# Turning attention probabilities on VectorE, through DRAM, for 24 of 32 head pairs

## The chip, the cores and the metric

One core of a Trainium2 chip runs the whole program. The metric is the device time of one execution in microseconds (us), as the median of several runs. The engines are TensorE (PE, with PEld for its weight loads), VectorE (DVE), ScalarE (ACT), GpSimd (POOL) and SyncE (SP), which only issues DMAs here.

## What is computed

Two attentions per head are added up and go through a gated spatial unit (batch 8, 8 heads, 576 tokens, head width 64):

```python
q_d, k_d, v_d = means over groups of 4 tokens        # 144 rows each
out_d  = softmax(q_d @ k_d.T / 8) @ v_d               # "downsampled"
mask   = abs(i - j) < 4                               # a band of 7 tokens
out_l  = softmax(where(mask, q @ k.T / 8, -1e9)) @ v  # "local"
x      = repeat(out_d, 4) + out_l                     # heads side by side: 576 x 512
h      = relu(x @ w_in);  u, v = h[:, :512], h[:, 512:]
v_n    = (v - mean(v)) / sqrt(var(v) + 1e-6)          # over channels
out    = (u * (w_spatial @ v_n + b_spatial)) @ w_out
```

## The kernel before

The work goes in head pairs (two heads on 2 x 64 partitions), four pairs per batch and 32 in all, and in one block of matrix products per batch, `gated(b)`, which needs the four pairs of its batch. The weights are loaded, decoded from 64-bit floats and split into two f16 halves at the start, beside the first pairs.

A pair (`attention(n)`) loads q and k transposed (`qk`), sums groups of four tokens (`sum1`, `sum2`, on DVE or POOL), and makes scores in PSUM. The local scores go in ten windows (`WS`) of 64 queries by 64 keys, two windows stacked on 128 partitions, five blocks of two: 128 x 640. `QB` says which queries of a window are used. The band mask is either added by two matmuls (PE) or by DVE. Then come the maximum, the subtraction on DVE (or folded into ten small exponentials of ACT), the exponential, the sum, its inverse and the normalisation. The downsampled scores are 144 x 144 per head, in three parts of 112 partitions, with the same steps (names with `d`).

The product with the values needs the probabilities with keys on partitions. So PE turns them: `turn` makes five 128 x 128 transposes (against `ident`) into a PSUM buffer `pa`, which ACT copies to `probT`; `turn_d` makes six transposes of 112 x 100 (against `perm`) into two PSUM buffers `pm`, which ACT copies to `pdT` (a single buffer). Then `values` and `values_d` multiply with v, DVE adds both results (`both`), and the sum is split into two f16 halves `x`. From pair 8 on (`MERGE`) the two kinds of scores are one piece of PE's order, and `values_d` with `values` another.

Every piece of work is handed to a planner (`plan.op`) with its engine, its cost in ns, the buffers that it reads and writes, and a rank. `Plan.run` goes through the program in its own time, and on each engine takes, among the pieces that can start within `NEAR` ns, the one with the lowest rank; that gives the order in which each engine's instructions are written. A DMA is given 1900 ns, then `kb` ns one after another, then 900 ns. Each engine, SP too, works in this fixed order, so an instruction that waits holds all behind it. `ON` picks for each pair, by a letter (P POOL, D DVE, A ACT, T PE), where a step runs; past the end of a string its last letter holds. Until 110 us the planner fills PE's gaps with matmuls that compute nothing (`warm`).

Of the kernel before, what the change touches and what calls it, by code (L numbers as in the profile page):

```python
# [8 lines left out]
F32 = mybir.dt.float32  # L9
# [67 lines left out]
class Plan:  # L77
# [61 lines left out]
    def run(self, near=150.0, stay=0.0, dma=(1900.0, 900.0), emit=True):  # L139
# [17 lines left out]
        while left:  # L157
# [122 lines left out]
MRANK = {"V": [[-120.813, 103.137], [-373.166, -785.223], [-588.287, 86.439], [-457.053, -295.554], [-271.069, 53.075],  # L280
            [-161.929, 7.172], [-384.75, 67.584], [1.753, -86.54]],
        "U0": [[-381.018, 507.475], [-225.844, -398.15], [392.079, 353.99], [415.277, -261.891], [-69.09, -16.703], [-362.251,
            -497.795], [59.314, -190.411], [573.297, -308.684]],
        "S0": [[631.14, 127.639], [-206.013, -184.383], [299.174, 561.899], [-372.357, 30.262], [381.875, 239.103], [33.324,
            19.169], [-136.587, -125.569], [104.744, -531.737]],
        "U1": [[66.951, 205.966], [432.921, 80.243], [202.58, -320.842], [-584.875, -261.385], [85.111, -539.421], [-290.079,
            -515.53], [-73.151, -407.568], [-105.893, -362.577]],
        "O0": [[170.632, -34.982], [-172.469, 696.573], [159.95, -390.053], [-841.668, -359.026], [22.932, -667.87], [-349.956,
            231.605], [321.827, -73.48], [-54.093, -578.395]],
        "S1": [[-122.247, -1002.997], [272.521, 179.124], [-502.627, -34.942], [83.425, -28.324], [193.115, 251.294], [212.725,  # L290
            -514.576], [-0.655, 14.458], [254.101, -410.908]],
        "O1": [[-425.021, 297.386], [239.962, 469.652], [56.568, -208.235], [-194.872, 129.628], [-641.125, -6.104], [281.584,
            274.929], [184.644, 89.516], [19.298, 376.248]]}
EVICT = 456.633
WRANK = {"WV load": [31.22, -21.921, 242.309, 4.474],
        "WV decode": [350.543, -287.444, -567.367, 661.466],
        "WV bound": [-83.736, 162.235, 909.503, 36.755, -835.361],
        "WV split": [-201.598, 11.031, -341.826, -1007.43],
        "WU load": [-364.293, 427.826, 390.089, -59.831],
        "WU decode": [387.574, -316.232, 1019.795, 459.568],  # L300
        "WU bound": [1425.684, -228.293, 245.85, 118.051, 725.352],
        "WU split": [-187.848, -607.313, -258.771, -328.661],
        "WSP load": [289.708, -579.107, 622.627, -316.354, 744.76],
        "WSP bound": [397.382, 106.669, -930.598, 200.751, 873.332, -382.338],
        "WSP split": [-150.625, -91.686, 309.424, 430.824, -1165.74],
        "WO load": [201.774, -325.888, 429.457, 987.307],
        "WO decode": [137.835, 619.019, -225.889, -8.083],
        "WO bound": [-64.148, 457.463, -289.1, 18.247, -58.582],
        "WO split": [620.04, -563.746, 894.059, 1022.164]}
NEAR = 104.496  # L310
STAY = 26.882
# [21 lines left out]
def tile_kernel(ctx, tc, qk, vw, v4, w_in, wT, bsp, w_out, out, emit=True):  # L333
# [75 lines left out]
    more = const.tile([P, 2, 2 * FF], F32, name="more")  # L409
# [9 lines left out]
    places("kd", 3, [P, 2, G], F32)  # L419
# [26 lines left out]
    places("mb", 6, [P, FF], F32)  # L446
# [254 lines left out]
    def attention(n):  # L701
# [16 lines left out]
        sb, kb = plan.buf("sum"), plan.buf("kd")  # L718

# [4 lines left out]
        def sum2():  # L724
            side(s2).tensor_tensor(kb.ap, sb.ap[:, :, ::2], sb.ap[:, :, 1::2], op=ALU.add)
# [7 lines left out]
        merge = n >= MERGE  # L733
# [73 lines left out]
        def scores_d():  # L807

            q = kb.ap.rearrange("p x g -> p (x g)")
            for h, a, i, e in ((0, 0, 0, 0), (0, 1, 1, 0), (1, 1, 0, 2), (1, 2, 1, 2), (0, 2, 0, 1), (1, 0, 1, 1)):  # L810
                r, o = slice(h * 64, h * 64 + 64), slice(i * 64, i * 64 + 64)
                nc.tensor.matmul(third(e)[o], q[r, a * 48:a * 48 + 64], kb.ap[r, 1], start=True, stop=True)
# [74 lines left out]
        def turn_d():  # L889
            for kc in range(2):  # L890
                v = ptd[kc].ap[:KEYS, :3 * PD].rearrange("p (a q) -> p a q", a=3)
                for a in range(3):
                    nc.tensor.transpose(v[:, a, :], ed.ap[:PD, a, kc], perm[:PD])
# [358 lines left out]
```

## Time and profile before

| | us |
|---|---|
| median of 3 runs | 579.25 (578.70 to 579.31) |
| span of the profiled execution | 577.2 |
| PE busy | 553.0 (96%) |
| DVE busy | 411.4 (71%) |
| ACT busy | 376.0 (65%) |
| POOL busy | 186.0 (32%) |

The median is 2.05 us above the profiled span. [...] A row of a timeline says start, duration, engine, line, operation, output and inputs, and how many instructions are merged. A row by line says how many instructions, their busy time, the mean ns of one, and the idle time before them. Matmuls overlap, so that PE's next instruction can start before the last has ended. The granted clock falls short of 1.00 only in the first 50 us (0.93).

### The profile page before, as it was taken

The page shows a single profiled execution, that of the slowest core. Times are in us where ns is not written, and L with a number is a line of the kernel's source. Part 1 is how long each engine was busy: PE and PEld are TensorE (multiplying, and loading weights), DVE is VectorE, ACT ScalarE, POOL GpSimd, SP SyncE. Part 2 cuts the span into 40 slices and gives each one's busy share as a digit, 9 for nine tenths or more (in the row PEclk, how much of TensorE's full clock was granted, in tenths as well). Part 3 has the DMA queues.
Part 4 walks back from the last instruction along what each step waited for, and adds up shares of the span by engine and source line. Part 5 has one row for each costly group of instructions (what it writes and reads, how often), then busy time and mean ns, then how long its engine had stood idle before and what let it go on. Part 6 is the DMA issues. An engine that isn't in the chain of part 4 may idle for free.

```text
span 577.2 us, 16026 instructions
## 1 busy us (share of the span) xinstructions
PE 553.0 (96%) x6501; PEld 368.2 (64%) x6501; DVE 411.4 (71%) x1062; ACT 376.0 (65%) x1076; POOL 186.0 (32%) x213
## 2 busy tenths in 40 slices
PE   5887899999999999999999999999999999999996
PEld 2455557764786566765776747778567567756752
DVE  6989899963898788677688776781976666844420
ACT  3689999457677678467565777565756665954422
POOL 3626532033431343254330432322422352203100
PEclk9899999999999999999999999999999999999999
DMA  8997970034423344234304443224230400000012
GB/s 286 336 256 213 214 171 2 0 118 128 105 66 103 104 107 122 66 108 120 86 20 135 102 95 102 84 77 112 62 102 0 139 2 19 11 29 2 20 55 74
DMA packets 37390, 57.04 MB, mean 99 GB/s; under 512 B 3650, under 2 KB 24130, under 8 KB 37316
## 3 DMA queue, kind: packets, MB, share of 16 engines
q1 hardware_dynamic: 35012, 48.94, 27.1%
q0 software_dynamic: 2304, 7.08, 7.3%
q8 instruction: 51, 0.84, 0.6%
q14 instruction: 23, 0.19, 0.1%
HBM read 46.57 MB, written 9.44 MB: 97 GB/s over the span
## 4 chain that ended last, share of the span: by engine, by line
PE 71%; DVE 14%; ACT 7%; DMA 5%; issue 1%; SPq 1%; POOL 1%; ACTq 0%; DVEq 0%
PE pmd L1126 4%; PE pma L1126 4%; PE pmb L1162 4%; PE pma L1162 4%; PE pmc L1031 4%; PE pmc L1162 4%; PE pma L1031 4%; PE pmc L1126 3%; PE pmb L1126 3%; PE pmd L1031 3%; PE pmd L1094 2%; PE pma L1094 2%; PE pmc L1094 2%; PE pmb L1031 2%; PE pmd L1162 2%; PE pmb L1094 2%
## 5 line engine op out<-in xcount | busy, mean ns | idle before, releaser
L1094 PEld LDWEIGHTS <-win 128*128 128x128 f16 x768 | 74.7, 98 | 20.6 <-issue 0.6
L1126 PEld LDWEIGHTS <-vha 128*128 128x128 f16 x768 | 74.0, 98 | 20.3 <-issue 1.9
L1162 PEld LDWEIGHTS <-gb 128*128 128x128 f16 x264 | 25.5, 98 | 28.5 <-issue 0.4
L1126 PE MATMUL pma<-wsp,vha 128*128 128x256 f16 (+1 forms) x216 | 29.4, 286 | 0.0
L1126 PE MATMUL pmd<-wsp,vha 128*128 128x256 f16 (+1 forms) x204 | 27.6, 285 | 1.1 <-DVE aua L1107 1.1
L1206 PE MATMUL pma<-mask_b,mask_a 128*128 128x512 bf16 x83 | 25.0, 438 | 3.1 <-DVE mask_a L383 3.1
L1126 PE MATMUL pmb<-wsp,vha 128*128 128x256 f16 (+1 forms) x180 | 24.1, 283 | 0.0
L1126 PE MATMUL pmc<-wsp,vha 128*128 128x320 f16 (+1 forms) x168 | 23.5, 290 | 0.0
L1162 PE MATMUL pmb<-wo,gb 128*128 128x512 f16 x96 | 22.0, 379 | 0.0
L1162 PEld LDWEIGHTS <-ga 128*128 128x128 f16 x120 | 11.6, 98 | 12.8 <-issue 0.2
L1059 POOL TENSOR_TENSOR sta<-sta,mhalf 128x1 f32<-128x1 f32 (+1 forms) x14 | 9.0, 646 | 32.8 <-DVE sta L1043 32.8
L1206 PEld LDWEIGHTS <-mask_a 128*128 128x128 bf16 x85 | 8.2, 108 | 13.8 <-issue 5.7
L671 POOL DMA_DIRECT2D tvb<-v_dram x12 | 10.8, 898 | 18.6 <-DMA tvb<-v_dram 14.1
L1162 PE MATMUL pma<-wo,gb 128*128 128x512 f16 x72 | 16.5, 379 | 0.0
L1031 PEld LDWEIGHTS <-xa 128*128 128x128 f16 x96 | 9.2, 98 | 10.9 <-issue 0.2
L671 POOL DMA_DIRECT2D tva<-v_dram x12 | 11.0, 919 | 13.7 <-DMA tva<-v_dram 9.7
L722 POOL TENSOR_TENSOR suma<-qka 128x576 f32<-128x576 f32 x6 | 7.1, 1190 | 23.2 <-DMA qka<-qk_dram 23.2
L1059 POOL TENSOR_TENSOR stb<-stb,mhalf 128x1 f32<-128x1 f32 (+1 forms) x15 | 10.9, 724 | 11.3 <-DVE stb L1043 11.3
L1162 PE MATMUL pmc<-wo,gb 128*128 128x512 f16 x60 | 13.8, 379 | 0.0
L1059 POOL TENSOR_TENSOR stc<-stc,mhalf 128x1 f32<-128x1 f32 (+1 forms) x11 | 7.2, 658 | 18.4 <-DVE stc L1043 14.8
L864 POOL TENSOR_SCALAR smdb<-smdb 112x3 f32<-112x3 f32 x3 | 0.6, 200 | 38.6 <-ACT eda L860 38.6
L722 POOL TENSOR_TENSOR sumb<-qkb 128x576 f32<-128x576 f32 x6 | 7.5, 1248 | 17.0 <-DMA qkb<-qk_dram 16.8
(1081 smaller groups left out, 1720.2 us busy)
## 6 DMA issues: line engine op xcount, KB each, us to landing
qka<-qk_dram SPq DMA_DIRECT2D x15, 576.0 KB, 5.2
qkb<-qk_dram SPq DMA_DIRECT2D x15, 576.0 KB, 5.8
tva<-v_dram POOLq DMA_DIRECT2D x12, 288.0 KB, 6.0
tvb<-v_dram POOLq DMA_DIRECT2D x12, 288.0 KB, 4.4
stg<-w_in_dram SPq DMA_DIRECT2D x5, 512.0 KB, 8.3
out_dram<-rowc SPq DMA_DIRECT2D x7, 256.0 KB, 2.1
out_dram<-rowb SPq DMA_DIRECT2D x7, 256.0 KB, 2.0
out_dram<-rowe SPq DMA_DIRECT2D x7, 256.0 KB, 2.0
```

Of the source, the lines that this page charges most:

```text
L671: plan.op("POOL", 850, lambda r=r: nc.gpsimd.dma_start(t.ap[LOW:KEYS], v4[b, r], accum_op=ALU.add), w=[t], rank=rank + 2.0 + 0.3 * r, kb=2 ...
L722: side(s1).tensor_tensor(sb.ap.rearrange("p x (g r) -> p x g r", r=2), x[:, :, :, :2], x[:, :, :, 2:], op=ALU.add)
L864: side(ivd).tensor_scalar(smd.ap[:PD], smd.ap[:PD], 1.0e-9, 4.0, op0=ALU.add, op1=ALU.mult)
L1031: nc.tensor.matmul(ps.ap, xs[c].ap[:, i, t * P:(t + 1) * P], win[:, c, j, FF:], start=(c == 0 and (i, j) == (0, 0)), stop=(c == NC - 1 and ...
L1059: plan.op("POOL", 530, lambda: nc.gpsimd.tensor_tensor(st.ap[:r, 8:9], st.ap[:r, 8:9], mhalf[:r], op=ALU.pow), w=[st], rank=rank - EVICT, ...
L1094: nc.tensor.matmul(ps.ap[:, :n], win[:, c, i, ft * P:(ft + 1) * P], xs[c].ap[:, j, HA[h]:HA[h + 1]], start=(c == 0 and (i, j) == (0, 0)), ...
L1126: nc.tensor.matmul(ps.ap[:, :n], vh.ap[:, c, i, fs], wsp[:, c, j, hs], start=(c == 0 and (i, j) == (0, 0)), stop=False)
L1162: nc.tensor.matmul(ps.ap, g.ap[:, c, HA[1] * i + k:HA[1] * i + k + P], wo[:, c, j, :], start=(c == 0 and (i, j) == (0, 0)), stop=(c == NF ...
L1206: nc.tensor.matmul(ap.rearrange("p (j k) -> p j k", k=64), mask_a, mask_b[:, None, :].broadcast_to([P, 8, 64]), start=True, stop=True)
```

## The change

From pair 8 on (`FLIP`), `turn` and `turn_d`, their PSUM buffers and ACT's copies are gone. DVE transposes the probabilities in blocks of 32 x 32 within SBUF (`turn_s`, `turn_e`); the blocks are then on the wrong partitions. SP writes them to scratch in DRAM with four and six DMAs (`hop_out`, `hop_out_d`; runs of 640 B, and of 256 or 128 B) and reads them back with one and three DMAs (runs of 2560 B) into `probT` and `pdL`. For that the groups of the downsampled queries lie in another order (`sum2`), all 128 partitions of `ed` are used, and `values` reads the moving operand in two runs (`across`). The new SBUF buffers lie where weights were staged (`mb`, `more`), so that the first flipped pair also waits for the weights (`after=weights`). All ranks, `NEAR`, `STAY`, `EVICT` and the picks of `ON` are new, and `QB[9]` is 520 instead of 518.

```diff
-RANK = {"load": [143.005, 47.751, 252.982, ...
+RANK = {"load": [1863.555, -4783.921, 3119.197, ...
...
-EVICT = 456.633
+EVICT = 1913.955
...
-NEAR = 104.496
-STAY = 26.882
+NEAR = 104.079
+STAY = 168.835
...
+FLIP = 8
...
-ON = {"sub": "DDDDDDADDADAAADDDADDAAADDDA",
-        "inv": "DDDDDPDDPDDPDPPDPDPDDPDPDDDPPPPD",
-        "invd": "DDDPDPPDDPDDDDDDPPDDPPDDDDPPPPD",
-        "sum": "DPPPDPPPDDPDPPDDDDPPDPDDDDPDDDPD",
-        "mask": "TTTTTTTTD",
-        "norm": "PDPPPDPDPPDDDPDPPPDPDPDPPPPDDPD",
-        "normd": "PAAPPDPPAAADDPAAPAPADAAPPPPADDAP",
-        "vlo": "PDPDPPPDDPDPDPDDDDPDDPPDDDPDPDDPDPDPDPD"}
+ON = {"sub": "DDADDDADDADAAADDDDDDDADDDADDADDD",
+        "inv": "DPDDDPDDPPPDDPPDDDDDDDDDDDDDPDPD",
+        "invd": "DDDDDPPDDDPPDDPPPPPDDPPDDDDPPDPD",
+        "sum": "PPPDDPPPDDPDPPDPPDPPPPDPDDPDDPDP",
+        "mask": "TDTTTTTTTDDDDTTDDDDDTDDDDDDDDDDD",
+        "norm": "PDPPDDPDPPDDDPDPDPPPPPPPPDPPDPPD",
+        "normd": "PAAPADPPADAPPPDAAAADDAAPAPADAAPP",
+        "vlo": "DDDPPPPDPPDDDDDDPDDDDPPDDDDDDDPPDPDDPDP"}
...
-    places("ed", 2, [P, 3, 2, KEYS], F32)
+    places("ed", 2, [P, 6 * KEYS], F32)
     for t in plan.places["ed"]:
-        nc.vector.memset(t[:, :, :, :LOW], 0.0)
+        nc.gpsimd.memset(t, 0.0)
...
+    places("hop", 3, [P, S + 64], F32, pool=dram)
+    places("hopd", 3, [32, 15 * P], F32, pool=dram)
+    plan.tag("yt", [late_place(f"mb{i}", f"yt{'ab'[i]}", [P, S + 64]) for i in range(2)])
+    plan.tag("yd", [late_place(f"mb{2 + i}", f"yd{'ab'[i]}", [P, S]) for i in range(2)])
...
+    plan.tag("pdL", [pd_place(0), pd_place(1)])
...
-        s2 = Way("sum", n, P=("POOL", 665, True), D=("DVE", 370, True))
+        s2 = Way("sum", n, P=("POOL", 900 if flip else 665, True), D=("DVE", 490 if flip else 370, True))
...
-        pt, pT = plan.buf("pa"), plan.buf("probT")
+        pt, pT = None if flip else plan.buf("pa"), plan.buf("probT")
+
+        def turn_s():
+
+            y = yt.ap.rearrange("p (g b q) -> p b g q", g=4, b=NBLK)
+            nc.vector.transpose(y, s.ap.rearrange("p (b h) (k q) -> p b (h k) q", b=NBLK, q=32))
+
+        def hop_out():
+            for a in range(4):
+                nc.sync.dma_start(hop.ap.rearrange("(g k) (a c) -> k a g c", k=32, a=4)[:, a],
+                                  yt.ap[a * 32:a * 32 + 32].rearrange("p (g c) -> p g c", g=4))
...
+        if flip:
+            yt, hop = plan.buf("yt"), plan.buf("hop")
+            plan.op("DVE", 740, turn_s, r=[s], w=[yt], after=weights if n == FLIP else (), rank=R["T"], name="T")
+            plan.op("SP", 1800, hop_out, lanes=4, r=[yt], w=[hop], rank=R["T"], kb=1200, name="hop")
+            plan.op("SP", 400, lambda: nc.sync.dma_start(pT.ap.rearrange("p j q -> p (j q)"), hop.ap), r=[hop], w=[pT], rank=R["T"], kb=900, name="hop2")
+        else:
...
-        ptd, pdT = (plan.buf("pm"), plan.buf("pm")), plan.buf("pdT")
+        ptd, pdT = None if flip else (plan.buf("pm"), plan.buf("pm")), plan.buf("pdL" if flip else "pdT")
+
+        def turn_e():
+            nc.vector.transpose(yd.ap.rearrange("p (b f q) -> p f b q", b=3, q=32), ed.ap[:, :6 * 96].rearrange("p (f b q) -> p f b q", b=3, q=32))
+
+        def hop_out_d():
+
+            to = hopd.ap.rearrange("k (m c) -> k m c", m=6)
+            for a, e, h, g, m in ((0, 0, 0, 0, 2), (1, 0, 0, 3, 2), (2, 1, 1, 0, 2), (3, 1, 1, 3, 2), (2, 0, 0, 2, 1), (0, 2, 1, 2, 1)):
+                x = yd.ap[a * 32:a * 32 + 32].rearrange("p (m c) -> p m c", m=6)
+                c = h * 160 + g * 32
+                nc.sync.dma_start(to[:, :, c:c + m * 32], x[:, :, e * 32:e * 32 + m * 32])
+
+        def hop_in_d():
+            for g in range(3):
+                k = 32 if g < 2 else KEYS - LOW - 64
+                nc.sync.dma_start(pdT.ap[LOW + g * 32:LOW + g * 32 + k], hopd.ap[:k, g * 640:g * 640 + 640])
...
+        if flip:
+            yd, hopd = plan.buf("yd"), plan.buf("hopd")
+            plan.op("DVE", 670, turn_e, r=[ed], w=[yd], after=weights if n == FLIP else (), rank=R["Td"], name="Td")
+            plan.op("SP", 2600, hop_out_d, lanes=6, r=[yd], w=[hopd], rank=R["Td"], kb=1600, name="hop")
+            plan.op("SP", 1200, hop_in_d, lanes=3, r=[hopd], w=[pdT.sub(0), pdT.sub(1)], rank=R["Td"], kb=900, name="hop2")
+        else:
...
+        def across(k, i, blk, q0, q1):
+
+            x = pT.ap.rearrange("p j q -> p (j q)")[k, i * 320 + blk * 32 + q0:]
+            return bass.AP(x.tensor, x.offset, [x.ap[0], [160 - q0, 2], [1, 32 - q0]])
...
+                if flip:
+
+                    q0, q1 = q0 - i * 64, q0 - i * 64 + QB[w + 1] - QB[w]
+                    z = min(q0, 64 - q1)
+                    nc.tensor.matmul(bank(two_v, blk % 2)[h * 64:h * 64 + 64, c + z - q0:c + 64 - z - q0], vb.ap[k, w], across(k, i, blk, z, 64 - z), start=True, stop=True)
+                    continue
```

## Rows read from the trace of the kernel before

**Rows 1.** Busy time, share of the span, instructions: PE of the page.
```profile
PE 553.0 (96%) x6501; PEld 368.2 (64%) x6501; DVE 411.4 (71%) x1062; ACT 376.0 (65%) x1076; POOL 186.0 (32%) x213
```
**Rows 2.** Engines by stage.
```profile
0.00:110.00 110.00, 93.46 (x1176) 57.36 (x1177) 97.70 (x245) 86.31 (x228) 47.32 (x64) 0.97 0.69 194
110.00:508.00 398.00, 395.30 (x4897) 272.24 (x4898) 291.25 (x760) 264.32 (x791) 131.82 (x141) 1.00 0.30 84
508.00:577.20 69.20, 64.21 (x440) 38.56 (x432) 22.44 (x61) 25.32 (x58) 6.84 (x8) 1.00 0.10 35
```
**Rows 3.** PE and PEld of one line: filler L1206, mask L743, values L954 (sum).
```profile
0.00:110.00 110.00, 25.65 (x85) 8.22 (x85) 0.97 0.69 194
...
0.00:110.00 110.00, 3.48 (x16) 1.48 (x16) 0.97 0.69 194
...
sum 577.20, PE 28.17 PEld 26.77; mean PE 9.39 PEld 8.92
```
**Rows 4.** Timeline of PE: the two kinds of turns and what follows.
```profile
298.52 0.71 PE L846 MATMUL pab<-ident,sb 128*128 128x128 f32 x5
299.06 0.60 PE L1126 MATMUL pmd<-wsp,vha 128*128 128x256 f16 x4
...
437.45 0.45 PE L893 MATMUL pmb<-perm,edb 112*100 112x112 f32 x3
437.74 0.45 PE L893 MATMUL pmc<-perm,edb 112*100 112x112 f32 x3
438.03 0.60 PE L1126 MATMUL pma<-wsp,vha 128*128 128x256 f16 x4
```
**Rows 5.** DVE by line and shape, 110 to 508 us.
```profile
L838 DVE TENSOR_TENSOR sa<-sa,smd 128x640 f32<-128x640 f32 x2 | 1.6, 820 | 1.4 <-POOL smd L801 1.4
L1046 DVE TENSOR_SCALAR rowc<-rowc,stc 128x512 f32<-128x512 f32 x1 | 1.6, 1573 | 0.0
L1046 DVE TENSOR_SCALAR rowb<-rowb,stb 128x512 f32<-128x512 f32 x2 | 1.1, 538 | 0.0
```
**Rows 6.** DVE of one line: L769, L782 (subtraction), L763 (mask), L722, L725 (sums).
```profile
110.00:508.00 398.00, 8.55 (x10) 1.00 0.30 84
...
110.00:508.00 398.00, 2.34 (x14) 1.00 0.30 84
...
110.00:508.00 398.00, 21.11 (x48) 1.00 0.30 84
...
110.00:508.00 398.00, 12.36 (x15) 1.00 0.30 84
...
110.00:508.00 398.00, 7.19 (x16) 1.00 0.30 84
```
**Rows 7.** Engines in two stretches of 50 us.
```profile
0.00:50.00 50.00, 38.79 (x512) 21.12 (x512) 40.79 (x98) 32.83 (x90) 23.25 (x39) 0.93 0.94 286
...
150.00:200.00 50.00, 49.61 (x708) 35.45 (x706) 44.76 (x120) 37.11 (x120) 14.93 (x15) 1.00 0.35 103
```
**Rows 8.** ACT of one line: copies of L848, copies of L896.
```profile
149.00:577.20 428.20, 16.27 (x24) 1.00 0.26 74
...
149.00:577.20 428.20, 16.15 (x46) 1.00 0.26 74
```
**Rows 9.** Timeline of SP's queue: a store, two loads behind a larger one.
```profile
364.42 0.35 SPq L1167 DMA_DIRECT2D out_dram<-rowc  x1
...
365.79 1.25 SPq L686 DMA_DIRECT2D va<-vw_dram  x2
```
**Rows 10.** DMA: packets, queue, and issues with median us to landing.
```profile
DMA packets 37390, 57.04 MB, mean 99 GB/s; under 512 B 3650, under 2 KB 24130, under 8 KB 37316
...
q1 hardware_dynamic: 35012, 48.94, 27.1%
...
qka<-qk_dram SPq DMA_DIRECT2D x15, 576.0 KB, 5.2
...
out_dram<-rowc SPq DMA_DIRECT2D x7, 256.0 KB, 2.1
...
vf<-vw_dram SPq DMA_DIRECT2D x4, 192.0 KB, 6.4
```

More of the change, by code (lines that the diff above doesn't have):

```diff
@@ L280 @@
[L280 to L293, printed above, removed]
@@ L445, in tile_kernel, with late_place, pd_place, make @@
     nc.gpsimd.memset(ones_b, 1.0)
-    places("mb", 6, [P, FF], F32)
+    plan.tag("mb", [const.tile([P, FF], F32, tag=f"mb{i}", name=f"mb{'abcdef'[i]}") for i in range(6)])
+    dram = ctx.enter_context(tc.tile_pool(name="dram", bufs=1, space=bass.MemoryType.DRAM))
+    def late_place(tag, name, shape):
+        return lambda: const.tile(shape, F32, tag=tag, name=name)
+    places("hop", 3, [P, S + 64], F32, pool=dram)
+    places("hopd", 3, [32, 15 * P], F32, pool=dram)
+    plan.tag("yt", [late_place(f"mb{i}", f"yt{'ab'[i]}", [P, S + 64]) for i in range(2)])
+    plan.tag("yd", [late_place(f"mb{2 + i}", f"yd{'ab'[i]}", [P, S]) for i in range(2)])
+    late_pd = []
+    def pd_place(i):
+        def make():
+            if not late_pd:
+                late_pd.append(const.tile([P, 2, 1024], F32, tag="more", name="pdL"))
+                nc.gpsimd.memset(late_pd[0][:LOW], 0.0)
+            return late_pd[0][:, i, :640]
+        return make
+    plan.tag("pdL", [pd_place(0), pd_place(1)])
     early = [const.tile([P, 2, S], F32, tag=f"w{i}", name=f"qk{'cd'[i]}") for i in range(2)]
@@ L807, in scores_d @@
         def scores_d():
-            q = kb.ap.rearrange("p x g -> p (x g)")
-            for h, a, i, e in ((0, 0, 0, 0), (0, 1, 1, 0), (1, 1, 0, 2), (1, 2, 1, 2), (0, 2, 0, 1), (1, 0, 1, 1)):
+            q, k = (kb.ap[:, :192], kb.ap[:, 192:]) if flip else (kb.ap[:, :2 * G], kb.ap[:, G:2 * G])
+            step = 64 if flip else 48
+            for h, a, i, e in ((0, 0, 0, 0), (0, 2, 1, 0), (1, 2, 0, 2), (1, 1, 1, 2), (0, 1, 0, 1), (1, 0, 1, 1)) if flip else \
+                    ((0, 0, 0, 0), (0, 1, 1, 0), (1, 1, 0, 2), (1, 2, 1, 2), (0, 2, 0, 1), (1, 0, 1, 1)):
                 r, o = slice(h * 64, h * 64 + 64), slice(i * 64, i * 64 + 64)
-                nc.tensor.matmul(third(e)[o], q[r, a * 48:a * 48 + 64], kb.ap[r, 1], start=True, stop=True)
+                nc.tensor.matmul(third(e)[o], q[r, a * step:a * step + 64], k[r], start=True, stop=True)
         pst, pdt = (ps.sub(0), ps.sub(1)) if merge else (ps, None)
@@ L892, in turn_d @@
                 for a in range(3):
-                    nc.tensor.transpose(v[:, a, :], ed.ap[:PD, a, kc], perm[:PD])
+                    nc.tensor.transpose(v[:, a, :], ed.ap[:PD, (2 * a + kc) * KEYS:(2 * a + kc + 1) * KEYS], perm[:PD])
         def copy_d(kc):
             nc.scalar.copy(pdT.ap[:, kc].rearrange("p (a i) q -> p a (i q)", i=2), ptd[kc].ap[:KEYS, :3 * PD].rearrange("p (a q) -> p a q", a=3)[:, :, :96])
-        plan.op("PE", 580, turn_d, r=[ed], w=list(ptd), hold=[pdT], rank=R["Td"], lag=PEL, mode="F", name="Td")
-        for kc in range(2):
+        if flip:
[4 more added lines that the diff above has]
+        else:
+            plan.op("PE", 580, turn_d, r=[ed], w=list(ptd), hold=[pdT], rank=R["Td"], lag=PEL, mode="F", name="Td")
+        for kc in range(0 if flip else 2):
             plan.op("ACT", 310, lambda kc=kc: copy_d(kc), r=[ptd[kc]], w=[pdT.sub(kc)], rank=R["Td"] - EVICT, name="copyTd")
@@ L943, in spread_d @@
                                      y[..., None].broadcast_to([*y.shape, 4]), start=(z == 0 and c == 0), stop=False)
-        order = [(blk, i, h) for j in range(0, NBLK, 2) for i in range(2) for blk in (j, j + 1) for h in range(2) if blk < NBLK]
+        order = [(blk, i, h) for j in range(0, NBLK, 2) for i in ((1, 0) if j + 1 == NBLK else (0, 1)) for blk in (j, j + 1) for h in range(2) if blk < NBLK]
+        def across(k, i, blk, q0, q1):
+            x = pT.ap.rearrange("p j q -> p (j q)")[k, i * 320 + blk * 32 + q0:]
+            return bass.AP(x.tensor, x.offset, [x.ap[0], [160 - q0, 2], [1, 32 - q0]])
         def values():
```

124 lines of the change are left out of this document (69 added, 55 removed), and 13 rows, old and new, of the table MRANK.

## The prediction

> **What bounds the kernel now.** I read the profile in four steps. First the busy times of the page: over the 577.2 us span TensorE (PE) is busy for 553.0 us [rows 1]. [...] So the middle stage, in which the last 24 of the 32 head pairs run beside the spatial unit, is bound by PE's work and by nothing else: it stands still for 2.7 us of 398. What is taken from PE there comes off the end; what is taken from another engine does not. Third, the turns themselves in PE's timeline [rows 4]. Fourth, the load of the engine and the transfers that take the turns over [rows 5 to 10].
>
> **The change part by part.**
>
> *Turns leave PE.* In one pair the five 128x128 turns of the local probabilities start at 298.52 us, and the matmul behind them starts at 299.06 us: 0.54 us. The six turns of the downsampled ones hold PE from 437.45 to 438.03 us: 0.58 us [rows 4]. I take these slots, not the busy times, because matmuls overlap. 24 pairs x (0.54 + 0.58) = 26.9 us off the path.
>
> *Work added on PE.* `ON` gives the mask to PE for pairs 8, 13, 14 and 20 and takes it away for pair 1. The mask matmuls of eight pairs took 3.48 us [rows 3], 0.44 us a pair; three more cost 1.3 us. The matmuls with the values get 588 columns a window set instead of 576 (from `across` and the new `QB`); all 32 pairs of them took 28.17 us [rows 3], so 2% over 24 pairs is 0.4 us. Net of PE: 26.9 - 1.7 = 25.2 us.
>
> *Work added on DVE.* Two 32x32 block turns per pair, over 640 and 576 columns. No row shows one. Nearest rows: a one-source pass over 512 columns takes 0.538 us, a two-source pass over 640 takes 0.820 us [rows 5]. Scaled, the two turns cost 0.67 + 0.61 = 1.28 us or 0.82 + 0.74 = 1.56 us; I take 1.4 us, between them. The far end is the one-source row with GpSimd's work beside it, 1.573 us [rows 5]: scaled to both turns, 3.7 us. They cannot cost less than nothing, since nothing of DVE's goes in exchange. 24 x 1.4 = 34 us, to 89 us at the far end. `ON` moves other work, priced by the means of [rows 6]: 7 more subtractions on DVE instead of folded into ACT's exponential, 7 x (0.86 - 0.17) = +4.8; 4 masks fewer, 4 x 0.88 = -3.5; 5 group sums fewer, 5 x (0.82 + 0.45) = -6.4; 3 normalisations fewer, 3 x 0.82 [rows 5] = -2.5. The other picks (`inv` +5, `invd` -3, `vlo` +2) leave four pieces that I bound by the same 0.82 us each, up to +3, and `sum2` goes in two instructions for 11 pairs, some +1 by the planner's costs in the diff (490 for 370 ns). Net -5 us, a little more or less. So DVE in the stage goes from 291 to 320 us, while the stage shrinks from 398 to 373: from 73% to 86% busy. From 150 to 200 us it was busy for 44.76 of 50 us and PE still for 49.61 [rows 7], so 86% can be borne; it costs something in queues. I put that at 2 us, about as much again as PE's idle time in the stage, with 0 and 17 us as ends (17 is worked out at the second rival).
>
> *Work removed from ACT.* One copy of 640 columns and two of 288 per pair: 16.27 us for 24 and 16.15 us for 46 recorded [rows 8], some 33 us in all; the seven folded exponentials that go back to one instruction save more. ACT is off the path; this counts nothing, but it lets PSUM be emptied sooner, which is why I don't put the DVE queues higher.
>
> *The moves.* Each flipped pair adds 14 DMAs to SP's queue: four out and one in for the local probabilities, six out and three in for the downsampled ones. SP's issues take 0.35 us (a store) or 0.63 us each (two behind a larger load) [rows 9]. 14 of them are 4.9 to 8.8 us, in a stage that has 373 / 24 = 15.5 us per pair. Queued behind them on SP: the loads of q, k and v for later pairs, and the output stores. A load into DRAM must land before SP issues the read back; while SP waits for that, these stand too. By bytes the moves are 328 + 328 + 246 + 184 KB = 1.09 MB per pair, 26 MB in all; by runs 512 of 640 B, 1152 of 128 or 256 B, and 200 of 2560 B, 44.7 thousand in all. SP's queue moved 48.94 MB in 35012 packets in 27.1% of sixteen engines' span [rows 10], 156 us of all sixteen. By bytes the moves take 83 us more, by packets 200 us. The stage now has a DMA share of 0.30 [rows 2], 119 us; afterwards 54% to 86% of 373 us. In the first 50 us the engines ran at 0.94 [rows 7], so that fits, but at the upper end transfers queue.
>
> *The trip.* From the probabilities to their use: now a turn and a copy; then a DVE turn, the issues out, a landing, the issues in, a landing. Landings: a store 2.1 us, a load of q and k 5.2 us, a v load of short runs 6.4 us [rows 10]. For the downsampled ones the short end is 0.7 + 6 x 0.35 + 2.1 + 3 x 0.35 + 2.1 = 8 us, the long one 0.7 + 6 x 0.63 + 6.4 + 3 x 0.63 + 5.2 = 18 us. `hop` and `hop2` enter the planner with 8 to 9 us for turn and trip (its due times, 1.9 + kb + 0.9 us each), so PE's order is built on the short end. I take the short end as a typical value, since most writes here are like the 2.1 us store and the stores are the only rows that go that way, and 1 us of PE waiting in all; the long end is the first rival. The buffers (two for `yt`, `yd` and `pdL`, three scratch areas) let a second pair go ahead of a late one.
>
> [...] The profile counts 3650 packets of under 512 B but shows no duration for them.
>
> [...]
>
> *Order and setup.* The ranks are all new. The first eight pairs and the weights keep their work, and DVE's 97.70 us of 110 [rows 2] leave at most 12 us to win there; I put it at nothing, with +-5 us. The flipped pairs wait for all weight work; the first turns of theirs come after 149 us, and the filler, which stands for waiting on weights, is all in the first 110 us [rows 3], so no cost. The larger clearing of `ed` moves to GpSimd, two instructions at the start.
>
> **The sum.** 577.2 - 25.2 + 2 (DVE queues) + 1 (trip) = 555.0 us of span. The median of the runs, 579.25 us, is 2.05 us above the profiled span; that lies around it and stays. Forecast: **557 us**, own range 547 to 563.
>
> **Rivals.**
> 1. *The trip comes late, and PE waits (slower).* PE runs in the planned order, so a late pair stops it at the matmuls with the values and holds all work of the spatial unit behind. At 18 us instead of 8 a pair is up to 10 us late; the order covers part of that with other matmuls. Waiting eats the whole gain at 25 / 24 = 1.05 us a pair. With 2 us a pair, a fifth of the possible lateness: 48 us, hence 554 + 48 = 602 us; 1.3 us a pair gives 585. For it: landings of 4 to 6 us are as frequent as short ones [rows 10], and SP's queue is in order. Against: DMA share is 0.30 now, and a pair has 15.5 us while the trip overlaps with other pairs. Chance 0.17.
> 2. [...] Chance 0.16.
> 3. *Front better by the new order.* Same mechanism, the front gains what DVE's idle time there allows, up to 12 us: 545 us. Chance 0.08.
> 4. *The turns were hidden anyway (no change).* It would need PE waiting for something else in the stage; 2.7 us idle of 398 speaks against it. 579 us, chance 0.04.
>
> **How the numbers follow.** Forecast 0.55, rivals 0.17, 0.16, 0.08 and 0.04. About 0.2% is what a measurement of this kernel can tell from no change, 1.2 us. Slower: rival 1, 0.17, and a little of rival 4, together 0.18. Same: 0.04. Faster: 0.78. The range reaches from the early side of rival 3 (545) through rival 2 to the near end of rival 1 (583), and leaves out the rest of rival 1 and a few percent below.
>
> **What would show it.** Right: in the middle stage PE's busy time falls by some 25 us and it stays above 98% busy; the two kinds of turns stand in DVE's list with means of 0.65 to 0.85 us; waits of PE for DMA into `probT` and `pdL` total a few us; DVE in the stage at 84 to 88%. Wrong: PE waits for those tiles in pair after pair (rival 1), with SP's issues or landings at 5 us and more; DVE's turns above 1 us and PE waiting for `u`, `x` or `s` from DVE (rival 2); a first stage of other length (rival 3).

## The result and the profile after

The changed kernel takes 560.69 us (median of 4 runs, 559.52 to 562.83) beside 579.28 us (578.70 to 579.79) for the kernel before: ratio 0.9685, 95% interval 0.9664 to 0.9706. The forecast was 557.0, with a range of 545 to 583. The gain is 18.6 us where 22.2 were forecast. A second set of runs of the same kernel gave 0.969 (0.9666 to 0.9714). A run that is over 1.5% above the fastest of its kernel is not counted in a ratio.

The page of the profiled execution, which took 559.52 us (against [rows 1] and [rows 10]):

```profile
span 557.7 us, 15970 instructions
...
PE 527.7 (95%) x6243; PEld 342.1 (61%) x6243; DVE 434.9 (78%) x1109; ACT 336.7 (60%) x956; POOL 188.8 (34%) x232
...
DMA packets 87312, 83.12 MB, mean 149 GB/s; under 512 B 36482, under 2 KB 69250, under 8 KB 87236
...
q1 hardware_dynamic: 84932, 75.01, 46.8%
```

A row by window has its start and end, its length, the busy us of PE, PEld, DVE, ACT and POOL, each with the number of instructions, the clock granted to PE as a share of the full one, the share of time in which the 16 DMA engines were busy, and GB/s. Where it is for one line, as in [rows 3], [rows 6] and [rows 8], the busy times are of that line alone. Engines by stage (against [rows 2]; the middle stage now ends at 488 us), and then the middle stage in four parts:

```profile
0.00:110.00 110.00, 92.52 (x1177) 57.38 (x1178) 93.09 (x242) 86.92 (x238) 44.20 (x62) 0.98 0.69 194
110.00:488.00 378.00, 370.14 (x4562) 244.10 (x4561) 316.27 (x800) 223.66 (x657) 137.83 (x162) 1.00 0.60 157
488.00:557.70 69.70, 65.03 (x507) 40.66 (x505) 25.52 (x68) 26.14 (x61) 6.79 (x8) 0.98 0.10 34
...
110.00:200.00 90.00, 86.12 (x1173) 56.45 (x1172) 78.13 (x193) 57.03 (x181) 42.92 (x49) 0.98 0.65 176
200.00:300.00 100.00, 96.02 (x1168) 63.21 (x1167) 83.69 (x211) 57.08 (x159) 38.38 (x47) 1.00 0.65 163
300.00:400.00 100.00, 100.00 (x1229) 65.39 (x1229) 87.96 (x228) 61.42 (x184) 32.31 (x39) 1.00 0.68 179
400.00:488.00 88.00, 88.00 (x1010) 59.04 (x1003) 66.49 (x170) 48.13 (x135) 24.21 (x28) 1.00 0.41 108
```

Two readings carry the result. PE's busy time fell from 553.0 to 527.7 us. And PE's idle time rose from 24.2 to 30.0 us: in the front from 16.5 to 17.5, in the middle stage from 2.7 to 7.9, at the end from 5.0 to 4.7. -25.3 + 5.8 = -19.5 us is the whole change of the span. The idle time of the middle stage lies before 300 us alone (3.9 + 4.0); from 300 to 488 us PE is busy for 188.00 of 188 us, with all turns on DVE and all moves going on.

What PE waited for in the middle stage (engine, tile and line, releaser; us in total, times, longest):

```profile
PE paa L997 <- ACT edb L913: 2.1, 1, 2.1
PE pma L1249 <- ACT ub L1184: 2.1, 1, 2.1
PE pmb L1213 <- ACT uf L1184: 1.3, 1, 1.3
PE pmb L1118 <- DVE rowb L1142: 1.2, 1, 1.2
...
PE pab L997 <- DMA pdL<-hopda: 0.2, 1, 0.2
```

Only 0.2 us are waits for a moved tile. The large ones are single waits for ACT: to empty a PSUM buffer with `relu` (`ub`, `uf`), or to have read the scores out of `paa` (the exponential of L913) before the next pair's values go there.

The two kinds of turns (DVE instructions of L874, local, and L944, downsampled: ns minimum, median, maximum):

```profile
L874 DVE STREAM_TRANSPOSE yta<-sc x4: 826/830/845, 131.0 to 386.0; 128x640 f32<-128x640 f32 x4
...
L944 DVE STREAM_TRANSPOSE yda<-eda x12: 729/776/780, 126.6 to 450.3; 128x576 f32<-128x576 f32 x12
```

Two of the waits for ACT follow one another. Rows of the timeline around them (start, duration, engine, line, operation; in brackets the idle time before and what ended it):

```profile
159.68 1.15 POOL L743 TENSOR_TENSOR sumb<-qkb 128x576 f32<-128x576 f32 x1 [0.45 <-PE pmc L840]
159.70 1.16 DVE L808 TENSOR_SCALAR mxd<-mxd 128x10 f32<-128x10 f32 x1
160.89 2.50 ACT L816 ACTIVATE sc<-sc,mxd 128x64 f32<-128x64 f32 x10 [1.46 <-DVE mxd L808]
163.48 0.52 ACT L1184 ACTIVATE uf<-pmb,sx2b 128x320 f32<-128x320 f32 x1
164.14 1.47 PE L1213 MATMUL pmb<-wsp,vha 128*128 128x256 f16 x12 [1.25 <-ACT uf L1184]
164.16 0.16 DVE L808 TENSOR_SCALAR mxa<-mxa 128x10 f32<-128x10 f32 x1
164.35 2.49 ACT L816 ACTIVATE sa<-sa,mxa 128x64 f32<-128x64 f32 x10 [0.26 <-DVE mxa L808]
166.18 0.17 DVE L908 TENSOR_SCALAR mxdd<-mxdd 128x3 f32<-128x3 f32 x1
166.75 0.36 ACT L913 ACTIVATE edb<-paa,mxdd 128x144 f32<-128x144 f32 x1
167.98 0.72 PE L997 MATMUL paa<-pdL,tva 64*64 64x144 f32 x16 [2.15 <-ACT edb L913]
169.42 2.73 PE L1213 MATMUL pmc<-wsp,vha 128*128 128x256 f16 x12
```

A DVE pass over ten columns takes 1.16 us beside a group sum on GpSimd that began 0.02 us earlier, and 0.16 us alone. ACT waits for it with its ten folded exponentials, 2.50 us in all; the `relu` of `uf` stands behind them in ACT's queue, and PE behind that. The pass ends within 0.03 us of GpSimd's sum. The new picks give GpSimd 13 of the group sums from pair 8 on, where it had 8. The wait for `ub` arises in the same way: at 222.18 us a DVE pass over 512 columns takes 1.15 us, instead of 0.54, beside a group sum of 1.14 us that began at 221.91, and ACT waits 1.62 us for it, ahead of the `relu`.

The wait for `paa` is another matter: the exponential of L913 starts at 166.75 us, when ACT's second ten folded exponentials (from 164.35, 2.49 us) are at their end, and 0.40 us after DVE's last pass for it. So an ACT free at that moment would have saved 0.40 of the 2.15 us; the rest is DVE's queue ahead of that pass, and the exponentials themselves.

After the waits for `uf` and `paa` the granted clock is low for some us, and full again behind it:

```profile
165.00:170.00 5.00, 2.85 (x68) 2.28 (x67) 4.07 (x12) 4.29 (x21) 1.82 (x3) 0.94 0.44 125
170.00:175.00 5.00, 5.00 (x109) 3.68 (x110) 4.88 (x16) 1.52 (x4) 1.06 (x2) 0.71 0.70 184
175.00:180.00 5.00, 5.00 (x63) 3.86 (x56) 4.07 (x11) 2.98 (x11) 0.00 (x0) 1.00 0.90 251
```

The twelve matmuls from 169.42 us take 2.73 us, where those from 164.14 us took 1.47. At 0.71 of the clock 5 us of busy PE are the work of some 3.6 us (an estimate from the granted clock), so 1.4 us more are lost, which stand in its busy time and not in its waits.

### The profile page after: what moved, and what is told of

It is laid out like the page before. It is cut to its first block, busy times and chain, and to the rows that moved or that the text cites. A ratio compares the mean times of both kernels' runs of the same rounds, so it can differ in the third digit from the quotient of the medians.

```text
span 557.7 us, 15970 instructions
## 1 busy us (share of the span) xinstructions
PE 527.7 (95%) x6243; PEld 342.1 (61%) x6243; DVE 434.9 (78%) x1109; ACT 336.7 (60%) x956; POOL 188.8 (34%) x232
## 4 chain that ended last, share of the span: by engine, by line
PE 49%; DVE 17%; ACT 11%; DMA 10%; SPq 8%; issue 3%; POOL 1%; ACTq 0%; DVEq 0%; POOLq 0%
SPq L952 4%; PE pmb L1213 3%; PE pmd L1249 3%; PE pmc L1181 3%; PE pma L1213 3%; PE pmc L1249 2%; DMA qkc<-qk_dram 2%; PE pmb L1249 2%; PE pmc L1213 2%; PE pmc L1118 2%; PE pmd L1213 2%; PE pma L1249 2%; PE pmd L1181 2%; PE pma L1181 2%; PE pmd L1118 2%
## 5 line engine op out<-in xcount | busy, mean ns | idle before, releaser
L1249 PEld LDWEIGHTS <-gb 128*128 128x128 f16 x240 | 23.0, 98 | 26.8 <-issue 1.1
L1213 PE MATMUL pmb<-wsp,vha 128*128 128x256 f16 (+1 forms) x216 | 29.1, 284 | 1.3 <-ACT uf L1184 1.3
L1213 PE MATMUL pmc<-wsp,vha 128*128 128x256 f16 (+1 forms) x204 | 28.6, 292 | 0.0
L1293 PE MATMUL pma<-mask_b,mask_a 128*128 128x512 bf16 x79 | 23.5, 439 | 3.5 <-DVE mask_a L385 3.5
L1213 PE MATMUL pma<-wsp,vha 128*128 128x320 f16 (+1 forms) x192 | 26.8, 289 | 0.0
L1213 PE MATMUL pmd<-wsp,vha 128*128 128x320 f16 (+1 forms) x156 | 21.4, 287 | 0.0
L743 POOL TENSOR_TENSOR sumb<-qkb 128x576 f32<-128x576 f32 x10 | 11.7, 1170 | 25.0 <-DMA qkb<-qk_dram 22.9
L1249 PE MATMUL pmd<-wo,gb 128*128 128x512 f16 x72 | 16.5, 379 | 0.3 <-ACT eda L913 0.3
L1249 PE MATMUL pmd<-wo,ga 128*128 128x512 f16 x72 | 16.5, 379 | 0.0
L743 POOL TENSOR_TENSOR suma<-qka 128x576 f32<-128x576 f32 x8 | 9.5, 1184 | 12.9 <-DMA qka<-qk_dram 12.9
L1249 PE MATMUL pmb<-wo,gb 128*128 128x512 f16 x60 | 13.8, 379 | 0.0
L1127 DVE BATCH_NORM_STATS2 stb<-rowb 128x6 f32<-128x512 f32 (+1 forms) x5 | 3.4, 689 | 11.1 <-ACT rowb L1136 10.8
```

Of the source, the lines that this page charges most:

```text
L743: side(s1).tensor_tensor(sb.ap.rearrange("p x (g r) -> p x g r", r=2), x[:, :, :, :2], x[:, :, :, 2:], op=ALU.add)
L1127: nc.vector.bn_stats(st.ap[:r, :6], vr.ap[:r])
L1213: nc.tensor.matmul(ps.ap[:, :n], vh.ap[:, c, i, fs], wsp[:, c, j, hs], start=(c == 0 and (i, j) == (0, 0)), stop=False)
L1249: nc.tensor.matmul(ps.ap, g.ap[:, c, HA[1] * i + k:HA[1] * i + k + P], wo[:, c, j, :], start=(c == 0 and (i, j) == (0, 0)), stop=(c == NF ...
L1293: nc.tensor.matmul(ap.rearrange("p (j k) -> p j k", k=64), mask_a, mask_b[:, None, :].broadcast_to([P, 8, 64]), start=True, stop=True)
```

## The experiments

Each is the changed kernel with one edit; ratios are against the kernel before, run beside it. Differences to the changed kernel are taken from its second set of runs, 560.37 us; the kernel before took 578.42 to 578.83 us beside the experiments.

**The changed kernel once more.**

> The changed kernel once more, beside the next three on the same chip, so that differences of 2 to 5 us can be told. Both theories: 559.5 to 562.8 us again.

Measured: 560.37 us (557.95 to 563.28, 6 runs), ratio 0.969 (0.9666 to 0.9714). In its profile PE is idle for 6.9 us of the middle stage. The waits are those above in other sizes (`uf` 2.0, `ub` 0.8, L997 1.1 us), so single waits of 1 to 2 us differ from run to run.

**Eight turns a pair back on PE.**

```diff
+        def back():
+            for _ in range(8 if flip else 0):
+                nc.tensor.transpose(bank(two_v, 1)[:, 384:512], ident, ident)
-  ... lambda: (values_d(), values()) ...
+  ... lambda: (values_d(), back(), values()) ...
```

> Eight 128x128 f32 turns of the identity per flipped pair are put back on PE, into unused columns of the PSUM buffer of the values, between values_d and values; order, DVE turns and moves stay. Eight turns of 0.109 us and the change of tile shape are 1.0 to 1.1 us a pair. Theory (PE's work still sets the end, so what left PE is the gain): 24 x 1.05 = 25 us more, 583 to 588 us, near the kernel before. Rival (DVE, SP's queue or the moves bind the stage now): PE has room, under 12 us more, 561 to 573 us.

Measured: 583.73 us (581.36 to 586.56), ratio 1.0091 (1.0065 to 1.0117): 23.4 us more. In the timeline of PE:

```profile
301.29 0.72 PE L997 MATMUL pab<-pdL,tva 64*64 64x144 f32 x16
301.94 1.09 PE L1030 MATMUL pab<-ident 128*128 128x128 f32 x8
302.96 0.74 PE L1043 MATMUL pab<-probTb,vd 64*64 64x64 f32 x34
```

The added turns have a slot of 302.96 - 301.94 = 1.02 us, times 24 = 24.5 us. PE's busy time rises by more, by 28.1 us (555.8 beside 527.7): the matmuls just before the turns hold it longer too, for 0.65 us (301.29 to 301.94) where it is 0.54 in the changed kernel (167.98 to 168.52). Its idle time falls by 3.1 us, and the profiled span is 25.0 us longer (582.7 beside 557.7). So most of what is put back on PE reaches the end, and the whole gain is gone, though all else of the change is still there. PE's work sets the end.

**Moves of almost no bytes.** All 14 DMAs of a pair stay, each with at most 32 runs of 64 B.

```diff
-  nc.sync.dma_start(to[:, :, c:c + m * 32], x[:, :, e * 32:e * 32 + m * 32])
+  nc.sync.dma_start(to[:, 0, c:c + 16], x[:, 0, e * 32:e * 32 + 16])
...                                   # the other 8 of the 14 in the same way
-                nc.gpsimd.memset(late_pd[0][:LOW], 0.0)
+                nc.gpsimd.memset(late_pd[0], 0.0)
```

> All 14 DMAs of a flipped pair stay, but each moves at most 32 runs of 64 B, so the turned probabilities don't arrive (part of the computation is left out); turns, order and PE's work stay. Theory (of the 5.2 us that PE stands still more in the middle stage than before, the late trip makes the most): the stage's idle time falls from 7.9 to under 4 us and the time by 3 to 6 us, 555 to 558 us. Rival (the idle time comes from DVE's and ACT's queues): within 1.5 us of the changed kernel, with the idle time still at 6 us or more.

Measured: 561.65 us (560.30 to 564.34), ratio 0.9717 (0.9696 to 0.9738). Its middle stage and the largest waits of PE there:

```profile
110.00:488.00 378.00, 368.26 (x4558) 244.22 (x4557) 313.92 (x804) 223.84 (x658) 137.81 (x162) 0.99 0.35 90
...
PE pmd L1180 <- ACT rowc L1135: 2.4, 1, 2.4
PE pmb L1212 <- ACT uf L1183: 2.2, 1, 2.2
PE pma L1248 <- ACT ub L1183: 2.1, 1, 2.1
PE paa L996 <- ACT edb L912: 1.7, 1, 1.7
```

The DMA share falls from 0.60 to 0.35 and PE is idle for 9.7 us, not less than 7.9: the waits for ACT are all still there. So the bytes and runs of the moves are not what PE waits for. The edit clears more of `pdL` (128 partitions, at 138.38 us on GpSimd), but that takes 1.81 us instead of 1.80 and hides no gain: from 150 to 300 us, behind the clearing, PE is idle for 8.2 us beside 7.8 in the changed kernel.

**Turns of almost no work.** DVE turns 32 columns instead of 640 and 576.

```diff
-  nc.vector.transpose(y, s.ap.rearrange("p (b h) (k q) -> p b (h k) q", b=NBLK, q=32))
+  nc.vector.transpose(yt.ap[:, :32], s.ap[:, 0, :32])
...                                   # turn_e in the same way
+            nc.gpsimd.memset(t, 0.0)  # once for each of the four buffers yt, yd
```

> DVE turns one 32-column block instead of 640 and 576 columns (part of the computation is left out); all moves, order and PE's work stay. This takes some 33 us from DVE in the middle stage, 84% to 75% busy. Theory of the late trip: the time stays within 1.5 us, or falls by at most 2 us because the moves start a little sooner. Rival (DVE's queue makes PE wait): 3 to 6 us less, 555 to 558 us, and PE's waits for rows and u shrink.

Measured: 562.91 us (561.55 to 564.54), ratio 0.9731 (0.9713 to 0.9750). Middle stage:

```profile
110.00:488.00 378.00, 368.14 (x4560) 244.53 (x4557) 288.91 (x806) 224.00 (x658) 144.37 (x166) 0.99 0.60 157
```

DVE is busy for 27 us less, and PE is idle for 9.9 us. Some of that idle time is the edit's own: GpSimd clears the four buffers between 131 and 149 us, DVE waits 3.2 and 2.7 us for two of them, and PE is idle for 1.7 us from 110 to 150 us, where it was for 0.05. Behind that, from 150 to 300 us, PE is idle for 8.2 us beside 7.8. So taking the turns' load from DVE gives nothing, and the turns themselves are not what is late either.

**Small group sums on GpSimd.** From pair 11 on GpSimd's group sums run over 4 and 8 groups only; most of the means of those pairs are left out, the rest is computed.

```diff
+  g = 4 if n >= 11 and s1.eng == "POOL" else G
-  x = qkb.ap.rearrange("p x (g r) -> p x g r", r=4)
+  x = qkb.ap.rearrange("p x (g r) -> p x g r", r=4)[:, :, :g]
...                                   # sum2: two sums over 8 columns
```

> From pair 11 on, GpSimd's group sums run over 4 columns instead of 576 and 288 (part of the computation is left out); order, turns and moves stay. Theory (what is left of PE's idle time comes from DVE's small passes that take 1.15 us instead of 0.16 or 0.54 while GpSimd sums, and from ACT's queue behind them): the waits of PE for uf and ub shrink from 1.3 and 2.1 to under 0.7 us each and the middle stage's idle time by 3 to 5 us; 556 to 558 us. Rival (ACT's own queue, the folded exponentials above all): idle time and waits as before, 559.5 to 562 us.

Measured: 558.13 us (554.68 to 560.06), ratio 0.9635 (0.9592 to 0.9679). Middle stage, waits, and the pass over ten columns:

```profile
110.00:488.00 378.00, 372.20 (x4609) 245.93 (x4610) 310.69 (x806) 225.69 (x660) 120.00 (x162) 1.00 0.60 158
...
PE paa L1002 <- ACT edb L918: 2.1, 1, 2.1
PE pab L1002 <- DMA pdL<-hopdb: 1.3, 1, 1.3
PE pmb L1218 <- ACT uf L1189: 0.8, 1, 0.8
...
161.82 0.18 DVE L813 TENSOR_SCALAR mxd<-mxd 128x10 f32<-128x10 f32 x1
```

The pass is back at 0.18 us, the wait for `ub` is gone and that for `uf` is 0.8 us; PE is idle for 5.8 us. The median is 2.2 us lower, but the intervals still overlap (0.9664 to 0.9679), so the size is not settled: 1 to 2 (against 6.9 and 7.9 us of idle time) of the 5.2 us that the stage's idle time grew by, and not the 3 to 5 expected. The wait of 2.1 us for `paa` stays.

**Two pairs with one exponential instead of ten.** Pairs 11 and 12, whose ten folded exponentials stand in the chain above, get their subtraction on DVE.

```diff
+        late_max = late_max and n not in (11, 12)
```

> Pairs 11 and 12 subtract on DVE and take one exponential instead of ten on ACT (2.5 us to 0.74 us of ACT, 0.16 to 0.82 us of DVE), in the same place of the same order. Rival (ACT's queue behind the two folded exponentials): PE's waits at 164 and 168 us (1.3 and 2.2 us) go and the clock doesn't dip at 170 us, 3 to 5 us less, 556 to 558 us. Theory of GpSimd's sums: the wait at 164 us stays, at most 2 us less, 558.5 to 561 us.

Measured: 558.56, 563.25 and 563.78 us in the runs that count (a fourth took 566.94), ratio 0.9709 (0.9663 to 0.9755). In the profile, of the fastest run, the wait for `uf` fell to 0.9 us, that for `paa` grew, and the granted clock still fell (0.66 from 170 to 175 us):

```profile
PE paa L998 <- ACT edb L914: 3.8, 1, 3.8
...
160.73 1.76 DVE L795 TENSOR_TENSOR sc<-sc,mxd 128x640 f32<-128x640 f32 x1
...
168.60 0.38 ACT L914 ACTIVATE edb<-paa,mxdd 128x144 f32<-128x144 f32 x1 [1.25 <-DVE mxdd L909]
```

No gain shows: a wait shortened at one place comes back at the next. The edit doesn't single out ACT's queue, though. It gives DVE a subtraction that takes 1.76 us beside the same group sum, where the ten-column pass took 1.16, and now ACT stands idle for DVE before the exponential that `paa` waits for. What the folded exponentials cost alone stays open.

**Each DVE turn twice.**

```diff
+  for _ in range(2):
       nc.vector.transpose(...)          # at both places
```

> Each of the two DVE turns of a flipped pair is made twice (same result), 1.6 us more of DVE per pair, 38 us in all: DVE's work in the middle stage goes from 316 us to some 354 of 378 us, 94%. Theory (DVE is near, but PE still sets the end): up to 10 us more, 562 to 571 us. Rival of the prediction (DVE becomes the bound): most of the 38 us shows, 580 to 600 us.

Measured: 581.44 us (580.40 to 587.40), ratio 1.0051 (1.0026 to 1.0075): 21 us more for 24 x (0.83 + 0.77) = 38.4 us of work added on DVE, 55% of it. The time lies at the near end of the rival's range. DVE is busy for 350.05 of the 398 us from 110 to 508 us, 88%. The largest waits of PE from 110 to 488 us are now spread over many places:

```profile
PE pmc L1183 <- ACT ua L1186: 2.6, 1, 2.6
PE pmb L1120 <- DVE rowb L1144: 2.5, 1, 2.5
```

I had expected little. DVE's free 16% of the stage are no margin: what is added to it delays PE by more than half. (The second turn also starts the moves some 0.8 us later; how much of the 21 us comes from that, no run here shows.)

**The six writes of the downsampled probabilities twice.** The second copy goes to an area that nobody reads.

```diff
+  ...                                # hopd twice as large, to[z, ...] its halves
+  for z in (1, 0):
-      nc.sync.dma_start(to[:, :, c:c + m * 32], x[:, :, e * 32:e * 32 + m * 32])
+      nc.sync.dma_start(to[z, :, :, c:c + m * 32], x[:, :, e * 32:e * 32 + m * 32])
```

> The six DMAs out of the downsampled probabilities are issued twice, the second time into scratch that nobody reads: the trip gets 3.6 us longer, SP's queue 24 x 3.6 = 87 us fuller, the runs under 512 B twice as many. Theory (the order has a few us to spare for the trip): under 10 us more, 561 to 571 us. Rival of the prediction (a late trip stops PE pair after pair): 24 x 3.6 = 87 us at most, over 590 us.

Measured: 584.79 us (583.71 to 587.38), ratio 1.0112 (1.0083 to 1.0142): 24.4 us more, 1.0 us a pair on average. The result lies between the two expected ranges. The issues took less than was expected (median 0.44 us, instead of 0.60; at 427.89 us seven in a row took 3.40 us): from the start of a pair's first write to the end of its last it is 7.05 us (median) instead of 3.94, so the trip got 3.1 us longer, not 3.6. Waits of PE:

```profile
PE paa L998 <- DMA pdL<-hopdc: 3.6, 1, 3.6
PE pab L998 <- DMA pdL<-hopda: 2.9, 4, 1.9
...
```

Now PE does wait for the moved tiles, at some places and not in every pair. On average 2.1 of the 3.1 us do not reach the end. The second copies load the DMA engines too (6 MB more in all), so that the trip's length is not the only thing that changed.

**The same bytes in long runs.** The six writes put the same bytes into scratch in runs of 1536 and 768 B, so that the blocks are read back in another order, and the downsampled part is left out.

```diff
+  ...                                # o = 0 ahead of the loop
-  nc.sync.dma_start(to[:, :, c:c + m * 32], x[:, :, e * 32:e * 32 + m * 32])
+  nc.sync.dma_start(hopd.ap[:, o:o + m * 192], yd.ap[a * 32:a * 32 + 32, :m * 192])
+  o += m * 192
```

> The same 246 KB per pair go out in the same six DMAs, but in runs of 1536 and 768 B instead of 256 and 128 B (blocks land in other places, so the downsampled part is not the right one). Theory (trip and DMA engines are not on the path): within 2 us of the changed kernel, 558.5 to 562.5 us, though the DMA share of the middle stage falls below 0.5 and an issue takes under 0.6 us. [...]

Measured: three runs of 557.30, 558.85 and 562.11 us, ratio 0.9667 (0.9628 to 0.9707); a fourth took 3044.17 us and is left out; what made it so long, no run here shows. The DMA part of the page, the six writes, and behind them those of the changed kernel:

```profile
DMA packets 64272, 83.12 MB, mean 150 GB/s; under 512 B 8834, under 2 KB 46210, under 8 KB 64196
...
q1 hardware_dynamic: 61892, 75.01, 45.7%
...
L952 SPq DMA_DIRECT2D hopda<-yda x24: 302/421/1894, 127.4 to 404.4; - x24
```

```profile
L952 SPq DMA_DIRECT2D hopda<-yda x24: 556/602/1666, 127.4 to 408.3; - x24
```

With 23040 packets fewer the time of all sixteen engines falls from 261 to 254 us: 7 us, or some 5 ns of one engine for each packet spared. An issue falls from 0.60 to 0.42 us, though not by its runs alone, as the doubled short writes were issued in 0.44. The DMA share of the middle stage is 0.58, and not below 0.5 as expected. The time is the same within its interval: the short runs add 7 us to the time of the sixteen engines, and nothing that shows at the end.

**No flip, and a flip from pair 20 on**, each planned anew with the ranks of the changed kernel.

```diff
-FLIP = 8
+FLIP = 99        # and 20 in the second
```

> FLIP = 99: the changed kernel's ranks, picks, QB and buffers, but every pair turned on PE as before; the planner lays the order out anew from the new ranks. Theory (the turns are the gain, the new order is not): PE gets its 26.9 us of turns back, 580 to 592 us. Rival (the new order and picks are the gain): 558 to 568 us.

> FLIP = 20: only the last 12 pairs are turned on DVE; the planner lays the order out anew. Theory (1.1 us of PE per flipped pair): about halfway between the changed kernel and the one without flipped pairs, 13 us more than the changed kernel, 570 to 577 us. Rival (the order): no relation to the number of pairs.

Measured: 615.02 us (613.44 to 616.26) and 602.95 us (598.04 to 606.91), ratios 1.0626 (1.0605 to 1.0647) and 1.0415 (1.0356 to 1.0473). PE's longest single wait is 6.7 us in the first and 8.8 us in the second, both for ACT.

Both lie above every expected range, and both are slower than the kernel before, though the first has all its turns where that kernel has them: the ranks seem to fit only the program that they were searched for. These two measure the fit of the order, not the change, and tell only that the new order alone does not make the gain. What the turns on DVE would give in the old order, no run here shows.

## Why the prediction was right, and where it was short

- **PE's slots** (25.2 us net): right. Busy time fell by 25.3 us, and with 28.1 us put back the time rose by 23.4. Masks cost 1.77 us for four pairs (0.44 each, as taken), and the values 21.32 us for 24 pairs against 20.85 before (the 960 matmuls from 144 us on), +0.5 instead of +0.4.
- **DVE's turns** (1.4 us a pair): too low. 0.83 + 0.77 = 1.60 us, the two-source price, just above the upper of the two near bounds. DVE's busy time in the stage still grew by only 25.0 us, where 29 were forecast: added up one by one, its instructions grew from 330.8 to 361.3 us, so that all but the turns fell by 8 us, not 5, and some 5 us more lie under other instructions, as DVE's overlap in the trace too (the one of 0.45 us from 166.25 us ends 0.08 us after the next has begun). At 83.7% of the stage it is about as busy as forecast, just below the sign of 84 to 88%.
- **DVE queues, 2 us, and trip, 1 us**: the mis-sized terms. The stage's idle time grew by 5.2 us, not 3, and its parts were others; at 97.9% busy PE also just missed the sign of 98%. Waits for the trip were 0.2 us (1.2 and 0.6 us in the second profile). The rest went to ACT's queue, held by DVE passes that GpSimd's sums stretched, and to a PSUM buffer that ACT had not yet read. The prediction took ACT for off the path, and its copies' removal for a relief; it did not look at what stands behind one wait in ACT's order. That the sums hold `uf` and `ub` up is read in the timeline; 1 to 2 us of the time point to them, by one experiment whose interval overlaps. The wait for `paa` stays with small sums, and what would remove it, no run here shows.
- **The sum**: the span is 557.7 us instead of 555.0. 2.2 us of the 2.7 lie in the middle stage, 0.9 in the front, the end gives 0.3 back, and -0.1 is PE's work (in which the estimated 1.4 us of low clock are contained). The median lies 3.0 us above the profiled span instead of 2.05, as the runs of the changed kernel spread over 3.3 us. Together 3.7 us.
- **The moves**: 26.1 MB in 49.9 thousand packets were added, against 26 and 44.7 forecast. Sixteen engines' time grew from 156 to 261 us, by 105, closer to the 83 us by bytes than to the 200 by packets; DMA share 0.60 of 0.54 to 0.86.
- **The trip of 8 us**: wrong, though the term that was taken from it, 1 us of waiting, came out. One pair's downsampled probabilities, from the turn to their use:

```profile
185.80 0.77 DVE L944 STREAM_TRANSPOSE ydb<-edb 128x576 f32<-128x576 f32 x1
...
216.35 3.82 SPq L952 DMA_DIRECT2D hopdc<-ydb  x6
...
221.76 1.17 SPq L957 DMA_DIRECT2D pdL<-hopdc  x3
...
232.94 0.72 PE L997 MATMUL pab<-pdL,tvb 64*64 64x144 f32 x16
```

  Over the 24 pairs it takes 7.2 to 38.4 us from the start of the turn to the end of the last read's issue (median 23.5; over 18 us in 16 pairs). Most of that is standing in SP's queue, up to 30.5 us before the first write; from the first write on it is 6.4 to 16.8 us (median 9.3). PE hardly waits because the order puts the use late, 18.5 to 47.1 us behind the turn and at least 2.3 us behind the last read's issue. A small term was right by the room in the order, not by the short trip that was given as the reason.
- **Rival 1** (trip late) did not come, but its point of decision is real: 1.05 us a pair eats the gain, and with a trip 3.1 us longer it was 1.0 us a pair and the gain was gone. Most trips were past the long end of 18 us all the same: what decides is the room between the last read and the use, not the length.
- **Rival 2** (DVE as the bound) did not come, since no turn was stretched to 1.5 us; but "86% can be borne" read too much from [rows 7]. Doubled turns, 1.6 us a pair, cost 21 us, with DVE at 88% and well before it is full. No run shows the 17 us that the prediction has as the far end of the DVE queues; these 21 us are what the runs show. The price of 1.573 us is not a single one: six passes of that line took 1.26 to 1.57 us in the kernel before, each beside GpSimd. The turns are just not stretched: 22 of the 48 ran beside a GpSimd instruction for over 0.3 us, and the longest of all took 0.85 us.
- **Rival 3** did not come: PE's idle time in the front rose by 0.9 us. The first turn of the flipped pairs stands at 126.6 us, not behind 149: the prediction overlooked that in the kernel before the downsampled turns of pair 8 began at 129.4. **Rival 4**: excluded, PE's slots came off.

## What to carry to other kernels

On the engine that bounds a stage count the slots between instructions, and most of what is removed there comes off the end (25.3 us of work, 19.5 of the span). How much room another engine or a transfer has is not read from its busy share or its length, but from the order: 84% busy was no margin, taking its load away gave nothing, and trips of over 20 us stopped nothing. So both sides have to be tried. An order that was searched for one program is part of that program; undo a part with the order kept, as with the eight turns, or the order is what is measured.

## What the runs showed of the hardware

- A DVE 32x32 block turn of f32 cost about as much as a two-source pass: 0.83 us for 128x640 and 0.77 us for 128x576 (medians), where a two-source pass over 640 columns took 0.82 us and a one-source pass over 512 took 0.54 us [rows 5]. Beside GpSimd it was not stretched (0.85 us at most).
- A DVE pass over ten columns took 1.16 us instead of 0.16 beside a GpSimd sum of 1.15 us, and one over 512 columns 1.15 us instead of 0.54 beside one of 1.14 us. With the sums made small the first took 0.18 us.
- The issue of one of the six short-run writes on SP took 0.60 us (192 runs of 128 or 256 B), with the same bytes in 32 runs 0.42 us, and 0.44 us where the short-run writes were issued twice.
- After waits of PE of 1.25 and 2.15 us, with 1.7 us of matmuls between them, the granted clock was 0.71 over 5 us, and twelve matmuls of 128x256 took 2.73 us instead of 1.47. In the second profile of the same kernel it fell behind the first wait, of 1.97 us: twelve matmuls took 2.30 us there instead of 1.47, and the granted clock was 0.58 and then 0.74, over 5 us each. A wait of 2.08 us by itself, which ended at 224.55 us, left it at 1.00 (225 to 230 us).
